# Eight transposes into a PSUM buffer of two banks, emptied by one copy of 1,024 columns, in a linear-attention and mixture-of-experts kernel

## The chip, the cores and the metric

The kernel runs on one core of one Trainium2 chip. The metric is the time of one execution on the device, in microseconds, as the median of several runs. Engine names in this text are those of the profile: PE is TensorE's matmul, PEld its weight load, DVE is VectorE, ACT is ScalarE, POOL is GpSimd, SP is SyncE, whose queue issues most DMAs.

## What is computed

Inputs: q, k, v, a_re, a_im of shape 4 (batch) x 8 (heads) x 768 (time) x 48; gate weights 384 x 8, noise, and eight experts' weights w1 (384 x 1024) and w2 (1024 x 384).

```python
scale = min(|a|, 0.999) / (|a| + 1e-6);  ar, ai = a_re*scale, a_im*scale
for t in range(768):                       # a complex state S of 48 x 48 for each batch and head
    S = (ar + i*ai)[:, None] * S + outer(k[t], v[t])
    y[t] = q[t] @ real(S)
x = y as 3072 rows of 384
logits = x @ w_gate + log1p(exp(x @ w_noise)) * noise
top 2 of 8 experts per row, softmax weights g
out[row] = sum over its 2 experts of g * (relu(x @ w1[e]) @ w2[e])
```

## The kernel before

The attention part takes the recurrence in chunks of 128 time steps: 6 chunks x 4 batches make 24 tiles (`NT`), and a group `g` is the 4 tiles of one chunk. A tile holds all 8 heads. Running products of a come from cumulative sums: PE multiplies logarithm and angle by triangular matrices (`p2t`, L250, and `p3`, L270, into the tile `cum`), and ACT takes exponentials and sines (`phase`, L199, with a load of another table, L198, at each switch between the two kinds). `p3q` (DVE, L282) makes from them q' and k' of a tile: 128 time steps by 8 heads by 112 numbers (`qh`, `kh`).

Then, for tile `n`:

- `tr_unit` (L286 to L294) transposes q' and k', so that the 112 numbers lie on partitions. Each call does 4 heads (a half): four PE transposes into one PSUM tile `ptr` of 4 x 128 columns, which is one bank, and one ACT copy of 512 columns into half of the SBUF tile `qT` or `kT`. There are four such calls for a tile: two halves of q', two halves of k'. The tile `ptr` has two buffers, as the pool `psA` has `bufs=2`.
- `sc_unit` (L302) multiplies k'T by q'T, 4 heads to a call, into `psc` (two buffers of one bank); DVE masks it into `am` (L303).
- `st_unit` (L312) makes the tile's addition to the state in `pG` (one bank), `y_unit` (L349, L351) the output in `pY` (one bank) from q'T and the state `z` and from `am` and v; ACT copies it to `xT` (L352).
- `x_unit`, `gate_logits` and `gate_dispatch` transpose the output back, find the two experts of each row and scatter the rows to the expert's places in DRAM by indirect DMAs (POOL, L413).

`cum` has two banks, `ptr` two, `psc` two, `pG` and `pY` one each: together the eight banks of PSUM.

The expert part then does, for each of 8 experts, transposes of the gathered rows (`x_T`, into `px`, L504; ACT casts, L506, and DVE takes the rest, L507), the first product (`mm1`, L519, into `ph`), and the second (`mm2`, L543). Its first pieces, expert 0 with 512 rows, run before the attention's PSUM pools close: `ps_tile` then gives `px` the buffers of `ptr` and `ph` those of `psc`.

The order of all this is not written out loop by loop. Every unit is put at a step by `at(step, function, ...)`, with offsets from the table `P`, and the units are traced in the order of these steps; a scheduler then places each engine's instructions by that priority and by when their operands and buffers are free. Each engine runs its own queue in the order that came out. The offsets of `tr_unit` are:

```python
at(n - P["tr"] + P["tk"] * i + P["th"] * half, tr_unit, n, i, half)   # tr=1.4, tk=0.2, th=0.05
at(n + P["sc"] + P["sh"] * half, sc_unit, n, half)                    # sc=-0.2, sh=0.05
at(n + P["st"], st_unit, n); at(n + P["y"], y_unit, n)                # st=0.05, y=0.2
```

Of the kernel before, what the change touches and what calls it, by code (L numbers as in the profile page):

```python
# [9 lines left out]
F32 = mybir.dt.float32  # L10
# [4 lines left out]
AF = mybir.ActivationFunctionType  # L15
# [62 lines left out]
def kernel(  # L78
# [8 lines left out]
    nc = tc.nc  # L87
# [28 lines left out]
    ident = cp.tile([128, 128], F32, name="ident")  # L116
# [47 lines left out]
    pa = ap.enter_context(tc.tile_pool(name="pa", bufs=1, side="right"))  # L164
# [5 lines left out]
    psA = ap.enter_context(tc.tile_pool(name="psA", bufs=2, space=PSUM))  # L170
# [112 lines left out]
                             QK[n][:, i, :].rearrange("p (h d) -> p h d", h=H)[:, None].to_broadcast([128, 2, H, D]),  # L283
                             tr)

    def tr_unit(n, i, half):  # L286
        x = (qh, kh)[i][n % NQ]
        store = (QT, KT)[i]
        if half == 0:
            store[n] = pa.tile([112, H, 128], F32, name=("qT", "kT")[i], bufs=2)  # L290
        p = psA.tile([128, 4, 128], F32, name="ptr")[0:112]
        for j in range(4):
            nc.tensor.transpose(p[:, j, :], x[:, 4 * half + j, :, :].rearrange("p r x -> p (r x)")[:, 0:112], ident)
        nc.scalar.activation(store[n][:, 4 * half:4 * half + 4, :], p, AF.Copy)  # L294

    def sc_unit(n, half):
        if half == 0:
# [128 lines left out]
    def at(step, f, *a):  # L426
        fill.setdefault(step, []).append((f, a))
# [37 lines left out]
    def ps_tile(name, bufs=2):  # L465
        if psB:
            return psB[0].tile([128, 512], F32, name=name, bufs=bufs)
        return psA.tile([128, 4, 128], F32, name={"px": "ptr", "ph": "psc"}[name]).rearrange("p a b -> p (a b)")


    def split(raw_t, hi, lo):
# [18 lines left out]
    def x_T(e, w):  # L490
        n = WIN[w][1]
        src_t = xga if w == 0 else xgb
        js = ((0, 1, 2, 3), (4, 5, 6))[w]
        if w == 0:
            GW[e] = mt([128, 7], F32, name="gw", bufs=2)
            OX[e] = mt([128, 7], U32, name="ox", bufs=2)
        nc.vector.tensor_copy(GW[e][:, js[0]:js[-1] + 1], src_t[:, :, DM + e])
        nc.vector.tensor_copy(OX[e][:, js[0]:js[-1] + 1], src_t[:, :, RNO])
        for kk in range(KD):
            x = XW[w, kk] = mt([128, 2, n], F32R, name=f"x{w}{kk}")  # L500
            p = ps_tile("px")
            for j in js:
                o = 128 * (j - js[0])
                nc.tensor.transpose(p[:, o:o + TW[j]], src_t[0:TW[j], j - js[0], kk * 128:(kk + 1) * 128],  # L504
                                    ident[0:TW[j], 0:TW[j]])
            nc.scalar.copy(x[:, 0, :], p[:, :n])  # L506
            nc.vector.tensor_tensor(x[:, 1, :], p[:, :n], x[:, 0, :].bitcast(F32), op=OP.subtract)  # L507

    def mm1(e, w, fs=range(KF)):
        n = WIN[w][1]  # L510
        for f in fs:

            h = mt([128, 2 * n], F32R, name=f"h{w}{f}")
            t = n % 128
            HT[w, f] = h[:, 0:n + t], h[:, n + t:]
            p = ps_tile("ph", 4)
            ms = [(i, j, kk) for kk in range(KD) for i, j in ((0, 0), (0, 1), (1, 0))]
            for m, (i, j, kk) in enumerate(ms):
                nc.tensor.matmul(p[:, :n], W1[kk][i][:, f * 128:(f + 1) * 128], XW[w, kk][:, j, :],  # L519
                                 start=(m == 0), stop=(m == len(ms) - 1))  # L520
            nc.scalar.activation(h[:, 0:n], p[:, :n], AF.Relu)  # L521
            for dst, a, b in ((n + t, 0, n - t), (n, n - t, n)):
                if a < b:
                    nc.vector.scalar_tensor_tensor(h[:, dst:dst + b - a], p[:, a:b], 0.0, h[:, a:b].bitcast(F32),  # L524
                                                   op0=OP.max, op1=OP.subtract)
# [9 lines left out]
    def mm2(e, w):  # L535
        for j in ((0, 1, 2, 3), (4, 5, 6) if e + 1 < E else (6, 4, 5))[w]:
# [8 lines left out]
            else:  # L545
# [15 lines left out]

    P = dict(la=10, p1=7, d1=1, p2=6, dt=0, ds=0, lqk=6, p3=4, d3=0, q=2, lv=5, xu=0.5, ss=3, gl=0, gd=0.25,
             tr=1.4, sc=-0.2, st=0.05, y=0.2, up=0.4, w1=18, w2=21, xt=23, m1=23.3, dm=0.2, co=6, hg=50,
             hx=50, hl=200, s0=(7, 5.5, 4.5), s1=(7.5, 6, 5), qd=0.05, tk=0.2, th=0.05, sh=0.05)
    pri = {gdis: P["hg"], x_unit: P["hx"], glog: P["hl"]}
    for g in range(NG):
        f = B * g + .5
# [8 lines left out]
        for j in range(B):  # L576
            n = B * g + j
# [5 lines left out]
    for n in range(NT):  # L583
        at(n + .5 - P["lv"], load_v, n)
        for i in range(2):
            for half in range(2):
                at(n - P["tr"] + P["tk"] * i + P["th"] * half, tr_unit, n, i, half)
        for half in range(2):
            at(n + P["sc"] + P["sh"] * half, sc_unit, n, half)
        at(n + P["st"], st_unit, n)  # L590
        at(n + P["y"], y_unit, n)
        at(n + P["up"], st_upd, n)
        at(n + .5 + P["xu"], x_unit, n)
        at(n + .5 + P["ss"], st_scale, n)
# [88 lines left out]
    nc.vector.tensor_add(flg[:, 1:2], flg[:, 1:2], flg[:, 0:1])  # L683
    nc.vector.tensor_add(flg[:, 1:2], flg[:, 1:2], ncnt)
    pfl = ps_tile("px")
    nc.tensor.matmul(pfl[0:1, 0:2], ones_f, flg, start=True, stop=True)
    flag = cp.tile([1, 2], I32, name="flag")
# [187 lines left out]
```

## Time and profile before

| | |
|---|---|
| median of 3 runs | 739.68 us (739.3 to 739.75) |
| the profiled execution | 739.76 us, of which the span from its first to its last instruction is 738.0 |
| attention tiles | about 32 to 257 us of the span |
| experts | from 257 us to the end |

The views that are used: busy time of each engine by stretches of the span; the view of one tile, which lists the instructions that touch it, what they waited for and who waited for them; the list of waits; groups of instructions by line and shape with their mean duration; and the timeline, in which each row is a run of equal instructions of one engine with its start, its length, its count and, in brackets, the idle time ahead of it and what ended that. An instruction that the program issues once for f32 operands stands as two passes in the trace where it is a product (L302, L312, L349, L351, L250, L270), and as one where it is a transpose (L293, L359, L504).

### The profile page before, as it was taken

What the parts mean: (1) busy time and instruction counts of PE and PEld (TensorE: products, weight loads), DVE (VectorE), ACT (ScalarE), POOL (GpSimd) and SP (SyncE); (2) the same over time, 40 slices, a digit from 0 to 9 for tenths busy, and PEclk for the clock granted to TensorE, in tenths of its full rate; (3) what the DMA queues carried; (4) which work ended last, traced back from release to release, by engine and by line L of the source; (5) the groups of instructions that cost most, each with busy time, mean ns of one, the idle gap of its engine ahead of it and who ended that gap; (6) DMA issues with size and microseconds to landing.
All of it is one profiled execution on the core that took longest, in us unless ns stands there. A gap on an engine that the chain in (4) does not pass through costs nothing. (4 is left out here: it accounts for less than half of the span.)

```text
span 738.0 us, 13470 instructions
## 1 busy us (share of the span) xinstructions
PE 699.7 (95%) x5184; PEld 622.5 (84%) x5184; DVE 411.3 (56%) x929; ACT 342.5 (46%) x609; POOL 166.1 (23%) x187
## 2 busy tenths in 40 slices
PE   0798989999999999999999999999999999999996
PEld 0377878878888879979988998998997998998995
DVE  5598888989899472553353344435525525435311
ACT  6899989798966430443133233223304403413300
POOL 2000005050506341032213123124024024122212
PEclk9899999999999999999999999999999999999999
DMA  7467876462457541271253244226226135031101
GB/s 284 118 222 189 263 218 239 132 219 46 155 143 238 201 165 74 81 239 51 97 172 106 87 139 147 75 98 202 75 88 208 43 115 191 28 108 54 51 33 34
DMA packets 64090, 100.18 MB, mean 136 GB/s; under 512 B 26490, under 2 KB 46129, under 8 KB 64016
## 3 DMA queue, kind: packets, MB, share of 16 engines
q1 hardware_dynamic: 54464, 71.68, 31.2%
q0 software_dynamic: 9552, 27.54, 10.7%
q8 instruction: 43, 0.70, 0.4%
q14 instruction: 31, 0.25, 0.1%
HBM read 68.55 MB, written 32.08 MB: 136 GB/s over the span
## 5 line engine op out<-in xcount | busy, mean ns | idle before, releaser
L543 PE MATMUL po<-w2h,h 128*128 128x384 f32 x768 | 201.8, 339 | 0.0
L519 PE MATMUL ph<-x,w1h 128*128 128x320 f32 (+1 forms) x720 | 192.4, 351 | 0.3 <-ACT x L506 0.3
L543 PEld LDWEIGHTS po<-w2h,h 128*128 128x128 f32 x768 | 139.9, 188 | 0.1
L519 PEld LDWEIGHTS ph<-x,w1h 128*128 128x128 f32 x720 | 126.7, 188 | 15.6 <-ACT x L506 0.5
L543 PE MATMUL po<-w2l,h 128*128 128x384 f32 x384 | 129.7, 338 | 0.0
L524 DVE SCALAR_TENSOR_TENSOR h<-ph,h 128x256 fp32r<-128x256 f32 (+2 forms) x184 | 74.2, 433 | 99.4 <-ACT h L521 99.4
L557 POOL DMA_INDIRECT out_dram<-ao,ox x56 | 55.7, 994 | 319.8 <-DVE ao L556 276.3
L519 PE MATMUL ph<-x,w1l 128*128 128x320 f32 (+1 forms) x360 | 125.5, 349 | 0.0
L521 ACT ACTIVATE h<-ph 128x320 fp32r<-128x320 f32 (+1 forms) x120 | 61.5, 512 | 119.0 <-PE ph L519 113.6
L556 DVE SCALAR_TENSOR_TENSOR ao<-po,gw,ao 128x384 f32<-128x384 f32 (+1 forms) x56 | 34.5, 616 | 134.0 <-PE po L543 133.0
L413 POOL DMA_INDIRECT xs<-xr,sl x48 | 53.7, 1118 | 200.6 <-DMA xd<-xr 108.6
L506 ACT CAST x<-px 128x320 fp32r<-128x320 f32 (+1 forms) x45 | 21.8, 502 | 126.8 <-PE px L504 125.9
L519 PEld LDWEIGHTS ph<-x,w1l 128*128 128x128 f32 x360 | 67.6, 188 | 7.3
L543 PEld LDWEIGHTS po<-w2l,h 128*128 128x128 f32 x384 | 72.1, 188 | 0.0
L530 POOL DMA_INDIRECT ao<-out_dram,ox x49 | 49.0, 1000 | 36.8 <-DMA out_dram<-ao,ox 24.0
L302 PE MATMUL psc<-qT,kT 112*128 112x128 f32 x384 | 53.3, 277 | 0.0
L472 ACT CAST w2h<-raw 128x768 fp32r<-128x768 f32 x32 | 25.3, 833 | 52.9 <-PE po L548 49.3
L302 PEld LDWEIGHTS psc<-qT,kT 112*128 112x128 f32 x384 | 47.7, 191 | 2.5 <-issue 1.3
L351 PE MATMUL pY<-am,v 128*48 128x128 f32 x384 | 42.6, 275 | 4.1 <-DVE am L303 4.1
L303 DVE TENSOR_TENSOR am<-psc,mask 128x512 f32<-128x512 f32 x48 | 32.6, 687 | 16.2 <-PE psc L302 16.1
L349 PE MATMUL pY<-qT,z 112*48 112x128 f32 x320 | 37.4, 276 | 0.0
L250 PE MATMUL cum<-t,tri_t 128*128 128x384 f32 x48 | 20.0, 545 | 17.6 <-ACT t L199 17.1
(206 smaller groups left out, 1019.6 us busy)
## 6 DMA issues: line engine op xcount, KB each, us to landing
raw<-in_moe_w_dram SPq DMA_DIRECT2D x24, 512.0 KB
raw<-in_moe_w_dram SPq DMA_DIRECT2D x32, 384.0 KB
qk<-in_qk_dram SPq DMA_DIRECT2D x24, 384.0 KB
xga<-xs SPq DMA_DIRECT2D x8, 800.0 KB
re<-in_a_dram SPq DMA_DIRECT2D x12, 384.0 KB
im<-in_a_dram SPq DMA_DIRECT2D x12, 384.0 KB
v<-in_v_dram SPq DMA_DIRECT2D x24, 192.0 KB
out_dram<-zero SPq DMA_DIRECT2D x12, 384.0 KB
```

Source lines behind the costliest of these rows:

```text
L302: nc.tensor.matmul(p[:, j, :], KT[n][:, h, :], QT[n][:, h, :], start=True, stop=True)
L303: nc.vector.tensor_mul(AM[n][:, 4 * half:4 * half + 4, :], p, mask[:, None, :].to_broadcast([128, 4, 128]))
L349: nc.tensor.matmul(o, Z[b][:, h, :], QT[n][:, h, :], start=True, stop=False, skip_group_check=True)
L351: nc.tensor.matmul(o, V[n][:, h, :], AM[n][:, h, :], start=not g, stop=True, skip_group_check=True)
L413: d = nc.gpsimd.indirect_dma_start(out=xs, out_offset=bass.IndirectOffsetOnAxis(ap=sl[:, kk, b:b + 1], axis=0), in_=XR[g][:, lo + b, :], i ...
L519: nc.tensor.matmul(p[:, :n], W1[kk][i][:, f * 128:(f + 1) * 128], XW[w, kk][:, j, :], start=(m == 0), stop=(m == len(ms) - 1))
L521: nc.scalar.activation(h[:, 0:n], p[:, :n], AF.Relu)
L524: nc.vector.scalar_tensor_tensor(h[:, dst:dst + b - a], p[:, a:b], 0.0, h[:, a:b].bitcast(F32), op0=OP.max, op1=OP.subtract)
L530: nc.gpsimd.indirect_dma_start(out=ao[j][0:w, :], out_offset=None, in_=out, in_offset=bass.IndirectOffsetOnAxis(ap=OX[e][0:w, j:j + 1], ax ...
L543: nc.tensor.matmul(p[:, :DM], HT[w, f][i][:, o:o + 128], W2[f // 2][k2][:, f % 2, :], start=(m == 0), stop=(m == len(ms) - 1))
L556: nc.vector.scalar_tensor_tensor(a, p[0:n, :DM], g, a, op0=OP.mult, op1=OP.add)
L557: nc.gpsimd.indirect_dma_start(out=out, out_offset=bass.IndirectOffsetOnAxis(ap=OX[e][0:n, j:j + 1], axis=0), in_=a, in_offset=None, bound ...
```

## The change

`tr_unit` loses its argument `half`: one call transposes all 8 heads of q' or k' into a `ptr` tile of 8 x 128 columns, which is two banks, and one ACT copy of 1,024 columns moves it to `qT` or `kT`. `ptr` now has one buffer, so that it takes the same two banks. `px` of the early `x_T` takes the first half of that one buffer. In the table `th` goes and `tk` is 0.4.

```diff
-    def tr_unit(n, i, half):
+    def tr_unit(n, i):
         x = (qh, kh)[i][n % NQ]
         store = (QT, KT)[i]
-        if half == 0:
-            store[n] = pa.tile([112, H, 128], F32, name=("qT", "kT")[i], bufs=2)
-        p = psA.tile([128, 4, 128], F32, name="ptr")[0:112]
-        for j in range(4):
-            nc.tensor.transpose(p[:, j, :], x[:, 4 * half + j, :, :].rearrange("p r x -> p (r x)")[:, 0:112], ident)
-        nc.scalar.activation(store[n][:, 4 * half:4 * half + 4, :], p, AF.Copy)
+        store[n] = pa.tile([112, H, 128], F32, name=("qT", "kT")[i], bufs=2)
+        p = psA.tile([128, H, 128], F32, name="ptr", bufs=1)[0:112]
+        for h in range(H):
+            nc.tensor.transpose(p[:, h, :], x[:, h, :, :].rearrange("p r x -> p (r x)")[:, 0:112], ident)
+        nc.scalar.activation(store[n], p, AF.Copy)
...
-        return psA.tile([128, 4, 128], F32, name={"px": "ptr", "ph": "psc"}[name]).rearrange("p a b -> p (a b)")
+        if name == "px":
+            return psA.tile([128, H, 128], F32, name="ptr", bufs=1).rearrange("p a b -> p (a b)")[:, 0:512]
+        return psA.tile([128, 4, 128], F32, name="psc").rearrange("p a b -> p (a b)")
...
-             hx=50, hl=200, s0=(7, 5.5, 4.5), s1=(7.5, 6, 5), qd=0.05, tk=0.2, th=0.05, sh=0.05)
+             hx=50, hl=200, s0=(7, 5.5, 4.5), s1=(7.5, 6, 5), qd=0.05, tk=0.4, sh=0.05)
...
-            for half in range(2):
-                at(n - P["tr"] + P["tk"] * i + P["th"] * half, tr_unit, n, i, half)
+            at(n - P["tr"] + P["tk"] * i, tr_unit, n, i)
```

The scheduler's order moves with it. Three places on PE, in which `x8` is the number of equal instructions in a row and the number behind `qh` or `kh` tells the two buffers of q' and k' apart.

The first tiles, on PE. Before:

```order
L293 MATMUL ptr<-ident,qh_123 112x128 x8
L312 MATMUL pG<-v,kh_125 48x48 x16
L293 MATMUL ptr<-ident,kh_125 112x128 x8
L293 MATMUL ptr<-ident,qh_124 112x128 x4
L302 MATMUL psc<-qT,kT 128x128
L293 MATMUL ptr<-ident,qh_124 112x128 x4
L302 MATMUL psc<-qT,kT 128x128 x3
L293 MATMUL ptr<-ident,kh_126 112x128 x4
```

and in the changed program:

```order
L292 MATMUL ptr<-ident,qh_123 112x128 x8
L311 MATMUL pG<-v,kh_125 48x48 x16
L292 MATMUL ptr<-ident,kh_125 112x128 x8
L292 MATMUL ptr<-ident,qh_124 112x128 x8
L301 MATMUL psc<-qT,kT 128x128 x8
L292 MATMUL ptr<-ident,kh_126 112x128 x8
```

Tile 1's transposes of q' now stand in one run right behind tile 0's of k', with nothing between them.

A late tile on PE, the last but two. Before, halves of k' and of the scores alternate:

```order
L293 MATMUL ptr<-ident,qh_123 112x128 x8
L302 MATMUL psc<-qT,kT 128x128 x4
L293 MATMUL ptr<-ident,kh_125 112x128 x4
L302 MATMUL psc<-qT,kT 128x128 x4
L293 MATMUL ptr<-ident,kh_125 112x128 x4
L349 MATMUL pY<-qT,z_566 48x128 x2
L351 MATMUL pY<-am,v 48x128 x2
```

In the changed program the next tile's place reads:

```order
L301 MATMUL psc<-qT,kT 128x128 x7
L292 MATMUL ptr<-ident,kh_126 112x128 x8
L348 MATMUL pY<-qT,z_638 48x128 x2
L350 MATMUL pY<-am,v 48x128 x2
L348 MATMUL pY<-qT,z_638 48x128 x2
L350 MATMUL pY<-am,v 48x128 x2
```

All eight scores of a tile now stand between the next tile's transposes of q' and of k', and the transposes of k' stand in one run ahead of the tile's output.

The start of the experts on PE. Before, seven of the first eight transposes of the gathered rows are one run, over both buffers:

```order
L504 MATMUL ptr<-ident,xga 128x128 x7
L399 LDWEIGHTS tri_b
L399 MATMUL cum<-ohs_3486,tri_b 128x8
L359 MATMUL cum<-ident,xT 128x128 x4
```

Now four, for the one buffer:

```order
L505 MATMUL ptr<-ident,xga 128x128 x4
L398 LDWEIGHTS tri_b
L398 MATMUL cum<-ohs_3390,tri_b 128x8
L358 MATMUL cum<-ident,xT 128x128 x4
```

The second group of transposes comes behind the first two products of `mm1`, which read the first group's result.

## Rows read from the trace of the kernel before

**Rows 1.** The page's first part: the span, and busy time, share and instructions of each engine.

```profile
span 738.0 us, 13470 instructions
PE 699.7 (95%) x5184; PEld 622.5 (84%) x5184; DVE 411.3 (56%) x929; ACT 342.5 (46%) x609; POOL 166.1 (23%) x187
```

**Rows 2.** Busy time of each engine by stretches (us from the span's start, then for each engine busy us and instructions, then the granted TensorE clock as a share, the DMA engines' busy share and GB/s).

```profile
50.00:100.00 50.00, 48.05 (x525) 38.82 (x525) 41.61 (x64) 46.26 (x82) 0.00 (x0) 1.00 0.68 203
100.00:150.00 50.00, 48.05 (x581) 40.65 (x577) 45.37 (x124) 42.12 (x80) 12.12 (x11) 1.00 0.65 204
150.00:200.00 50.00, 49.31 (x603) 42.60 (x603) 44.46 (x96) 45.87 (x82) 17.78 (x20) 1.00 0.44 137
200.00:250.00 50.00, 49.38 (x602) 43.15 (x600) 40.84 (x137) 32.81 (x67) 18.29 (x19) 1.00 0.64 202
...
262.00:738.00 476.00, 468.30 (x2590) 431.25 (x2590) 201.27 (x420) 132.65 (x234) 112.64 (x114) 1.00 0.33 106
```

**Rows 3.** The view of the tile `ptr`: its copies (count, then duration in ns least/median/most), what the engines that touch it waited for, and who waited for it.

```profile
L294 ACT ACTIVATE qT<-ptr x48: 586/597/661, 34.0 to 246.1; 112x512 f32<-112x512 f32 x48
L294 ACT ACTIVATE kT<-ptr x48: 577/597/670, 36.8 to 248.7; 112x512 f32<-112x512 f32 x48
...
  ACT kT L294: 1.7, 5
...
  ACT kT L294: 9.2, 17
  ACT qT L294: 1.9, 4
```

**Rows 4.** The waits of PE and of its weight loads from 30 to 262 us (in total, times, longest).

```profile
PE pY L351 <- DVE am L303: 4.1, 5, 1.3
PE cum L270 <- ACT ee L199: 3.8, 1, 3.8
PE cum L399 <- DVE ohs L392: 1.9, 3, 1.3
PE ptr L293 <- ACT kT L294: 0.5, 2, 0.3
...
PEld ptr L293 <- issue: 6.3, 29, 1.0
PEld ptr L293 <- ACT kT L294: 1.2, 3, 0.5
```

**Rows 5.** Groups by line and shape up to 340 us: copies on ACT of other widths (count, busy us, mean ns of one, idle before).

```profile
L360 ACT COPY xr<-cum 128x384 f32<-128x384 f32 x24 | 11.6, 484 | 5.2 <-PE cum L359 4.2 <-DMA raw<-in_moe_w_dram 0.9
L352 ACT ACTIVATE xT<-pY 128x512 f32<-128x512 f32 x24 | 14.3, 598 | 6.5 <-PE pY L351 6.5
L199 ACT ACTIVATE t<-t 128x768 f32<-128x768 f32 x36 | 29.7, 849 | 0.3
L472 ACT CAST w1h<-raw 128x1024 fp32r<-128x1024 f32 x6 | 6.2, 1045 | 0.0
```

**Rows 6.** The timeline of a late tile, 237 to 242.5 us, PE and ACT.

```profile
237.66 1.09 PE L293 MATMUL ptr<-ident,qh 128*112 128x128 f32 x8
238.34 1.08 ACT L294 ACTIVATE qT<-ptr 112x512 f32<-112x512 f32 x2
238.58 1.06 PE L302 MATMUL psc<-qT,kT 112*128 112x128 f32 x8
239.47 0.60 PE L293 MATMUL ptr<-ident,kh 128*112 128x128 f32 x4
...
240.81 0.60 PE L293 MATMUL ptr<-ident,kh 128*112 128x128 f32 x4
241.34 0.43 PE L349 MATMUL pY<-qT,z 112*48 112x128 f32 x4
241.45 0.60 ACT L294 ACTIVATE kT<-ptr 112x512 f32<-112x512 f32 x1 [0.58 <-PE ptr L293]
```

**Rows 7.** The timeline of a tile in the middle, 149 to 156 us, in which ACT is behind.

```profile
148.81 1.08 PE L293 MATMUL ptr<-ident,kh 128*112 128x128 f32 x8
149.50 0.60 ACT L294 ACTIVATE kT<-ptr 112x512 f32<-112x512 f32 x1 [1.30 <-PE ptr L293]
149.99 0.93 ACT L199 ACTIVATE t<-t,b_eps 128x768 f32<-128x768 f32 x1
150.15 0.65 PE L293 MATMUL ptr<-ident,qh 128*112 128x128 f32 x4 [0.25 <-ACT kT L294]
150.94 1.28 ACT L198 ACT_TABLE_LOAD   x1
152.23 1.58 ACT L199 ACTIVATE t<-t 128x768 f32<-128x768 f32 x2
153.72 0.58 ACT L294 ACTIVATE kT<-ptr 112x512 f32<-112x512 f32 x1
```

**Rows 8.** The timeline of two more pairs of copies, 96 to 116 us, ACT.

```profile
101.44 1.11 ACT L294 ACTIVATE kT<-ptr 112x512 f32<-112x512 f32 x2
104.55 1.14 ACT L294 ACTIVATE qT<-ptr 112x512 f32<-112x512 f32 x2
```

**Rows 9.** The timeline of PE in the first tiles, 40 to 62 us.

```profile
43.74 0.64 PE L351 MATMUL pY<-am,v 128*48 128x128 f32 x8 [0.89 <-DVE am L303]
45.94 1.41 PE L312 MATMUL pG<-v,kh 128*48 128x48 f32 x30 [0.47 <-DVE z L324]
58.10 1.50 PE L312 MATMUL pG<-v,kh 128*48 128x48 f32 x32 [0.65 <-DVE z L324]
```

**Rows 10.** The start of the experts, 256.5 to 262.5 us.

```profile
257.19 0.98 PE L504 MATMUL ptr<-ident,xga 128*128 128x128 f32 x7
258.36 0.57 ACT L506 CAST x<-ptr 128x512 fp32r<-128x512 f32 x1
259.01 0.69 DVE L507 TENSOR_TENSOR x<-ptr,x 128x512 fp32r<-128x512 f32 x1
261.07 0.66 PE L504 MATMUL ptr<-ident,xga 128*128 128x128 f32 x4
```

**Rows 11.** Short stretches of the start, columns as in the second group.

```profile
30.00:35.00 5.00, 5.00 (x23) 3.06 (x22) 5.00 (x7) 4.97 (x11) 0.00 (x0) 0.50 0.56 106
35.00:40.00 5.00, 4.75 (x56) 4.45 (x55) 5.00 (x9) 3.31 (x8) 0.00 (x0) 0.96 0.70 139
60.00:65.00 5.00, 3.89 (x32) 3.01 (x30) 5.00 (x7) 4.56 (x12) 0.00 (x0) 1.00 0.52 91
```

## The prediction

> **What bounds the kernel now.** Start from the page's first part [rows 1]: PE is busy for 95% of the span, ACT for 46%. Then the stretches [rows 2]. From 262 us on PE is busy for 468.3 of 476 us and ACT for 132.7, so the experts are PE's alone, and the change touches nothing there but their first transposes. Whatever it does is done before, in the 24 attention tiles, and moves the end of the program by as much. In that part PE's busy share is 96 to 99%, but ACT stands at 46.3 of 50 us in one stretch and 45.9 in another, DVE at 41 to 45. So three engines are close to full, and the question is which of them is waited for last. The waits answer it [rows 4]: between 30 and 262 us PE's matmuls stood still for named reasons for about a dozen us in all, mostly for the masked scores (4.1 us) and one exponential (3.8 us). For the copies that the change merges, PE stood still twice, 0.5 us, and its weight loads three times, 1.2 us. The other way round the copies waited for the transposes 21 times, 9.2 and 1.9 us [rows 3]. PE is the engine to watch, then, and today the copies hardly delay it: ACT's relief by itself has little to give, and a new wait of PE would be paid nearly in full.
>
> **Term 1, the copies.** 96 copies of 512 columns become 48 of 1,024. One of 512 takes 597 ns [rows 3]; 384, 512, 768 and 1,024 columns in other copies and functions take 484, 598, 849 and 1045 ns [rows 5]. From 512 on, 512 more columns at 0.77 ns each (768 to 1,024) give 0.99 us, at 0.89 ns (384 to 512) 1.05; I take 1.03. Two copies that follow each other take 1.08, 1.11 and 1.14 us from the first's start to the second's end [rows 6, 8], so a merged pair saves 0.05 to 0.11 us; at 0.08 the 48 pairs save 3.8 us of ACT. Where a copy stands alone, 0.597 x 2 - 1.03 = 0.16 us goes, at most 7.9 us for all. What reaches the end is that part in which PE waits for ACT in its turn. ACT is above 90% busy in two of the four attention stretches [rows 2], so I count half: -1.9 us, with 0 (all of it hidden under PE) and -3.8 as bounds.
>
> [...]
>
> **Term 2, TensorE's turns.** Changing from another kind of work to a run of transposes costs PE a little: weight loads of `ptr` began late 29 times with nothing that released them, 6.3 us, 0.22 us each [rows 4]. The order before enters a run of `ptr` transposes 81 times from other work, the changed one 70 times, since halves no longer alternate with scores. 6.3 / 81 x 11 = -0.9 us; bounds 0 and 11 x 0.22 = -2.4.
>
> **Term 3, one buffer.** This is what the change adds. Before, the third half could be transposed while the first was copied. Now the transposes of k' wait until the whole of q' is copied, and those of the next q' until k' is. In a quiet tile [rows 6] the last of four transposes starts 0.33 us behind the first (240.81), and the copy starts 0.64 behind the first, so 0.2 us after PE is free for other work; the copy is 1.03; and PE begins 0.05 us behind a copy's end (150.10 to 150.15 [rows 7]). So PE needs 1.28 us of other work between two runs of transposes, if ACT is free. Such work can be counted from the changed order: a transpose is 0.11 us, eight passes of scores 0.89 (238.58 to 239.47 [rows 6]), so all eight heads, 16 passes, 1.79, and 32 passes of `pG` 1.5 [rows 9].
>
> There are 47 hand-overs between the 48 runs. Thirty-one have 2.2 us or more of other work between them, up to 7, and hide the copy with room to spare. Thirteen have 1.29 to 1.85 us, typically the scores of one tile between the next tile's q' and k'. Three have less than the need: 0.00, 0.44 and 0.99 us. The three cost 1.28 + 0.84 + 0.29 = 2.4 us; the first falls into the filling of the pipeline, where PE stands still anyway for the masked scores and the state (0.89 and 0.47 us [rows 9]), so I count 1.1. Of the thirteen, four are in the last tiles, where copies start at once; they cost nothing. The other nine have some 0.5 us of room, and lose where ACT has an operation of 0.9 us or more ahead of the copy. In 75 of 96 copies ACT did not wait for PE [rows 3], and where it is behind it can be far behind: the second half of k' is transposed by 149.9 us and copied at 153.72, behind an activation, a table load and two more activations [rows 7]. But such long stretches meet the wide gaps of the changed order more than the thin ones. I take 0.2 us each, 1.8 us. Together +2.7; bounds 0 (ACT always free, fill hidden) and 2.4 + 9 x 0.5 = +6.9.
>
> Queued behind a waiting transpose is all of PE's work, as its queue runs in order; next in line are the scores, then DVE's mask, then the output.
>
> **Term 4, the experts' start.** Three groups of four transposes now share one buffer that is free only when ACT's cast and DVE's subtraction are through: 0.57 and 0.69 us [rows 10]. The order puts two products and other work between them, some 1.35 to 1.45 us, against a need near 1.5. I take +0.3, bounds 0 and +0.8. Before, the third group already had to wait until 261.07 [rows 10].
>
> The edits to `tk` and `th` have no cost of their own: they make the order that the terms count. DMA issues on SP and POOL are the same in number, and follow DVE and the tiles.
>
> **Sum.** -1.9 - 0.9 + 2.7 + 0.3 = +0.2 us on the profiled execution's 739.76, so 740.0; that execution stands 0.08 us above the median of the runs shown, which is no difference. About 0.2%, 1.5 us, is what a measurement of this kernel can tell from no change. So the forecast is no measurable change, 738.2 to 741.2, with a chance of 0.35.
>
> **Rivals.** *The relief arrives whole.* If ACT is what the attention tiles wait for in truth, through chains that the waits name otherwise (scores masked late because k' was copied late), then all of term 1 counts, term 2 at its estimate, and hand-overs hide under the scores as in the last tiles: -3.8 - 0.9 + 0.6 = 735.7 us. For it: ACT's 46 of 50 us, and copies up to 4 us behind [rows 2, 7]. Against it: 1.7 us of PE waits on copies. Chance 0.33.
>
> *The single buffer becomes the new wait.* It costs from the point at which ACT starts a copy more than about 0.5 us late at the thirteen thin hand-overs. Term 3 and 4 at their bounds, with relief and turns worth 2 us, give 739.8 + 6.9 + 0.8 - 2 = 745.5; half-way, 743. For it: PE waits for nothing else so directly. Against it: today many reuses of a buffer have as little room, and PE lost only 1.7 us by them [rows 4]. Chance 0.28. [...]
>
> *The merged copy is no cheaper.* If reading across two banks costs as much as two copies, 1.19 us, ACT gains nothing, and each copy is 0.11 us longer than an adjacent pair: half of 48 x 0.11 = +2.6 in place of -1.9, and thirteen hand-overs longer by 0.16: 740.0 + 4.5 + 2.1 = 746.6. No row shows a copy over two banks. Chance 0.03.
>
> *TensorE's clock falls.* [...] Chance 0.01. [...]
>
> **Numbers.** Faster by more than 0.2%: 0.33. Within: 0.35. Slower: 0.28 + 0.03 + 0.01 = 0.32. The range takes in the first rival's price with the forecast's lower bounds, and the second's up to its full price: 734.5 to 745.5. The forecast case's own range is 738.2 to 741.2.
>
> **What would show it.** Right: 48 copies of 0.99 to 1.05 us; ACT's busy time down by 3 to 8 us; PE's waits on `qT` and `kT` copies up from 1.7 to some 3 to 5 us; experts from about the same moment, 257 us. Wrong on term 3: those waits above 7 us, at the hand-overs with scores alone between. Wrong on term 1: waits of PE on masked scores and exponentials fall by several us, and the experts start before 254 us.

## The result

The changed kernel takes 746.03 us (median of 4 runs, 744.36 to 746.38), the kernel before 739.49 us (738.53 to 739.75) beside it: ratio 1.0087, 95% interval 1.007 to 1.0103. It is 6.5 us slower, above the range's upper end of 745.5. The profiled execution took 746.38 us with a span of 744.6.

**The profile after.** The page's first part, against [rows 1]:

```profile
span 744.6 us, 13412 instructions
PE 700.2 (94%) x5184; PEld 621.9 (84%) x5184; DVE 411.6 (55%) x929; ACT 338.5 (45%) x561; POOL 174.9 (23%) x187
```

ACT has 48 instructions and 4.0 us less, PE's work is the same. The view of the tile `ptr`, against [rows 3]:

```profile
L293 ACT ACTIVATE qT<-ptr x24: 1012/1024/1047, 33.5 to 243.6; 112x1024 f32<-112x1024 f32 x24
L293 ACT ACTIVATE kT<-ptr x24: 1002/1023/1056, 35.7 to 246.8; 112x1024 f32<-112x1024 f32 x24
...
  ACT kT L293: 4.0, 5
  ACT qT L293: 3.9, 3
```

The merged copy takes 1.02 us, and PE and its weight loads sat idle for such copies 7.9 us (4.0 and 3.9), before 1.7 for k' [rows 3] and 0.2 for q'. Still the attention is no longer. From the last copy of k' of the second tile to that of the last tile (41.85 to 248.65 us before, 40.61 to 246.84 after, the lines below) it is 206.80 us before and 206.23 after. What else differs up to here is the start of the execution, and that is not the change's: in the other runs, of both kinds of kernel, the second tile's copy stands anywhere from 40.3 to 42.0 us. Before:

```profile
41.85 0.59 ACT L294 ACTIVATE kT<-ptr 112x512 f32<-112x512 f32 x1
248.65 0.60 ACT L294 ACTIVATE kT<-ptr 112x512 f32<-112x512 f32 x1 [0.74 <-PE ptr L293]
```

and after:

```profile
40.61 1.02 ACT L293 ACTIVATE kT<-ptr 112x1024 f32<-112x1024 f32 x1 [0.17 <-PE ptr L292]
246.84 1.02 ACT L293 ACTIVATE kT<-ptr 112x1024 f32<-112x1024 f32 x1 [1.83 <-PE ptr L292]
```

The time goes at the seam, where the attention ends and the experts begin. The waits from 30 to 262 us, against [rows 4]:

```profile
POOL xr L339 <- DMA xs<-xr,sl: 13.3, 4, 5.8
DVE gw L498 <- DMA xga<-xs: 8.6, 1, 8.6
PE pY L350 <- DVE am L302: 8.0, 2, 7.2
PEld ptr L292 <- issue: 5.8, 25, 1.3
PE ptr L292 <- ACT kT L293: 1.7, 2, 1.1
PE ptr L292 <- ACT qT L293: 1.5, 1, 1.5
```

PE's one wait of 7.2 us is for the last tile's masked scores. The timeline of the seam (PE, PEld and DVE, with the issue of one load from SP's queue, SPq) shows who stands ahead of them. It stands against [rows 10], where the experts' first transposes began at 257.19 and their third group at 261.07:

```profile
251.52 0.86 PE L301 MATMUL psc<-qT,kT 112*128 112x128 f32 x6
...
253.23 0.39 PE L348 MATMUL pY<-qT,z 112*48 112x128 f32 x4
254.76 0.33 SPq L442 DMA_DIRECT2D xga<-xs  x1
259.08 0.17 DVE L498 COPY gw<-xga 128x4 f32<-128x4 f32 x1 [8.57 <-DMA xga<-xs]
260.03 0.68 DVE L302 TENSOR_TENSOR am<-psc,mask 128x512 f32<-128x512 f32 x1
260.77 0.67 PE L350 MATMUL pY<-am,v 128*48 128x128 f32 x4 [7.15 <-DVE am L302]
262.22 1.12 PE L505 MATMUL ptr<-ident,xga 128*128 128x128 f32 x4
266.18 0.66 PE L505 MATMUL ptr<-ident,xga 128*128 128x128 f32 x4
268.44 0.60 PE L505 MATMUL ptr<-ident,xga 128*128 128x128 f32 x4
```

Read it from DVE: `gw`, a copy of 0.17 us out of the rows gathered for expert 0 (`x_T`, L498), stands in DVE's queue ahead of the mask, and waits 8.57 us for the gather. Before it waited too, 2.38 us:

```profile
250.45 0.33 SPq L443 DMA_DIRECT2D xga<-xs  x1
254.71 0.17 DVE L497 COPY gw<-xga 128x4 f32<-128x4 f32 x1 [2.38 <-DMA xga<-xs]
255.66 0.68 DVE L303 TENSOR_TENSOR am<-psc,mask 128x512 f32<-128x512 f32 x1
```

The last scores were done at 252.38 (251.52 + 0.86), and their mask began only at 260.03, 7.65 us later, behind `gw`. The load itself did not get slower: from its issue to the start of `gw` it is 4.26 us before and 4.32 after. It was issued 4.3 us later.

Then the clock. Stretches of after, columns as in [rows 2]:

```profile
250.00:255.00 5.00, 3.62 (x56) 3.04 (x50) 0.51 (x1) 0.74 (x2) 1.94 (x2) 1.00 0.35 126
255.00:260.00 5.00, 0.00 (x0) 0.00 (x0) 0.59 (x5) 0.22 (x1) 0.00 (x0) 0.80 0.48 164
260.00:265.00 5.00, 4.23 (x31) 3.52 (x31) 4.09 (x25) 1.98 (x5) 0.00 (x0) 0.52 0.01 2
```

Behind a stop of 7 us PE works at a mean granted clock of 0.52 in these 5 us, and four transposes of the rows take 1.12 us instead of 0.66. In stretches of 1 us each from 245 to 295 us, PE's idle time is 8.15 us in all and the busy time lost to the lower clock (busy share times one less the clock, added up) 2.0 us; before the two were 1.45 and 0. That is +8.7 us (8.15 - 1.45 + 2.0); less 1.2 for the earlier start and 0.6 for the attention it is 6.9, against the 6.6 by which the spans differ.

### The profile page after: what moved, and what is told of

It reads as the page before. It is cut to its first block, busy times and chain, and to the rows that moved or that the text cites. A ratio compares the mean times of both kernels' runs of the same rounds, so it can differ in the third digit from the quotient of the medians.

```text
span 744.6 us, 13412 instructions
## 1 busy us (share of the span) xinstructions
PE 700.2 (94%) x5184; PEld 621.9 (84%) x5184; DVE 411.6 (55%) x929; ACT 338.5 (45%) x561; POOL 174.9 (23%) x187
## 5 line engine op out<-in xcount | busy, mean ns | idle before, releaser
L412 POOL DMA_INDIRECT xs<-xr,sl x48 | 63.0, 1312 | 193.4 <-DVE am L302 123.8
L301 PE MATMUL psc<-qT,kT 112*128 112x128 f32 x384 | 50.9, 277 | 0.5 <-ACT kT L293 0.5
L350 PEld LDWEIGHTS pY<-am,v 128*48 128x48 f32 x384 | 29.3, 124 | 12.7 <-DVE am L302 8.9
```

Of the source, the lines that this page charges most:

```text
L301: nc.tensor.matmul(p[:, j, :], KT[n][:, h, :], QT[n][:, h, :], start=True, stop=True)
L350: nc.tensor.matmul(o, V[n][:, h, :], AM[n][:, h, :], start=not g, stop=True, skip_group_check=True)
L412: d = nc.gpsimd.indirect_dma_start(out=xs, out_offset=bass.IndirectOffsetOnAxis(ap=sl[:, kk, b:b + 1], axis=0), in_=XR[g][:, lo + b, :], i ...
```

## Experiments

Two theories stood at first: **A**, the loss is a late gather and DVE's queue behind it; **B**, it is the hand-overs of the single buffer. The gather's chain is: gate of group 4 on DVE (slots `sl`, L408), eight scatters on POOL (L412), the load of `xga` on SP, `gw`. The slots are the places in DRAM to which the rows of the group go; a scatter needs them. Counted from the second tile's last copy of k', the slots stand 1.9 us later than before in the changed kernel's profile, but the first scatter of group 4 stands 5.7 us later (201.75 against 196.04). The other 3.8 are POOL's: that scatter stood behind a memset of POOL (L339) that waited for group 3's scatters, 5.77 us, until 241.52. In a_gw and a_free, whose programs are the same at this place, the memset ended near 239.3 and the first scatter began 1.5 to 1.8 us behind the slots, so this share differs from run to run.

**a_gw.** `gw` and `ox` behind the last mask in DVE's queue:

```diff
-        nc.vector.tensor_copy(GW[e][:, js[0]:js[-1] + 1], src_t[:, :, DM + e])
-        nc.vector.tensor_copy(OX[e][:, js[0]:js[-1] + 1], src_t[:, :, RNO])
+        c = nc.vector.tensor_copy(GW[e][:, js[0]:js[-1] + 1], src_t[:, :, DM + e])
+        d = nc.vector.tensor_copy(OX[e][:, js[0]:js[-1] + 1], src_t[:, :, RNO])
+        if (e, w) == (0, 0):
+            for i in (c, d):
+                tc.add_manual_dep(i.ins, LAST_AM[0].ins.name, mybir.DependencyInfo(
+                    mybir.DependencyClass.NoSync, mybir.DependencyReason.DATA), reason="behind the last mask")
```

> The changed kernel with one thing moved on DVE: the two small copies of expert 0's gathered rows (gw, ox out of xga) stand behind the last tile's mask instead of ahead of it. Theory A (the 6.5 us come from DVE's queue standing behind a late gather, not from the buffer): PE's wait of 7.2 us on the last am goes, the last tile's output is made at about 254 us; the gather itself still lands at about 259, so the experts start near 260 instead of 262.2 and the clock falls less: 741 to 744 us in place of 746.0. Theory B (hand-overs of the single buffer): 745.5 to 746.5, since nothing on the copies is touched.

Measured: 746.21 us, ratio 1.0106 (1.0092 to 1.0121). No gain, and outside A's 741 to 744; B's 746.5 is nearer. In its profile PE then waited for the gather itself, 0.76 us, and 1.6 us for `ohs` (the rows' choices of experts as ones and zeros, which PE sums to places), which DVE made behind `gw`.

**a_pad.** The memset and copy for group 5's `xr` behind group 4's scatters on POOL:

```diff
-            nc.gpsimd.memset(XR[g][:, :, RNO + 1:ROW], 0.0)
-            nc.gpsimd.tensor_copy(XR[g][:, :, RNO], tokid[:, g])
+            if g + 1 < NG:
+                pad_xr(g)
...
             at(B * g + hi + .5 + P["gd"], load_x, 0, 0, xga)
+            at(B * g + hi + .5 + P["gd"] + .05, pad_xr, NG - 1)
```

`pad_xr` holds the two lines, and for group 5 orders them behind the last scatter.

> The changed kernel with one thing moved on POOL: the memset and the copy that prepare the row buffer xr of group 5 (the last) stand behind group 4's scatters instead of ahead of them, so that these scatters don't wait for group 3's scatters to land. Theory A: group 4's first scatter at about 238 us instead of 242.4, the gather lands by 256, no wait over 3 us of PE on am, experts from about 256 to 257.5: 737.5 to 740.5 us. Theory B: 744.5 to 746.5, as the copies are as they were.

Measured: 744.73 us, 1.0087 (1.0072 to 1.0103). The scatters start at 240.0 instead of 242.4 us, and not at 238; the time is outside A's 737.5 to 740.5 and within B's range. The ratio is as without the move; its interval leaves room for about 1 us either way.

**a_both** and the control **b_both**: both moves, in the changed kernel and in the one before.

> The changed kernel with both moves, on DVE and on POOL. Theory A: the attention's own gain of about 1.8 us (the last copy of k' at 246.8 us against 248.6) comes through to the end: 736.5 to 739 us. Theory B: 744 to 746.5.

> The kernel before (halves, two buffers) with both moves, the control. Its gather was waited for by 2.4 us on DVE, and PE by about 1 us. Theory A: 0 to 1.5 us faster than before, 738 to 739.5, and the changed kernel with both moves is 0.5 to 2.5 us faster than this one. Theory B: this one is 5 to 7 us faster than the changed kernel with both moves.

Measured: 743.94 us, 1.0062 (1.0047 to 1.0076), and 737.05 us, 0.9977 (0.9965 to 0.9988). The control is 1.4 us faster than the kernel before, as theory A said. The changed kernel is far outside A's 736.5 to 739: 6.9 us are still between the two, within the 5 to 7 that theory B had asked for. So the memset and the place of `gw` are not the cause, only carriers, and B was not yet out. The gather still lands late (`gw` waits 3.1 us), and the first to the ninth transpose of the rows takes 9.7 us (3.9 before).

**a_free and b_free** take the gather out of the question, and leave out the right rows for expert 0's start. From here A is called theory **S** (all of the loss is the late gather at the seam), and a third theory stands beside it, **C** (the single buffer at the experts' start). Expert 0's first rows come from `v`:

```diff
-            at(B * g + hi + .5 + P["gd"], load_x, 0, 0, xga)
+            at(B * g + hi + .5 + P["gd"], load_free)
+    def load_free():
+        nc.sync.dma_start(xga[:, :, 0:DM], v[0:4].rearrange("j p r -> p j r"))
+        nc.sync.dma_start(rw, x3[0, 0:512, DM:RNO + 1].rearrange("(p j) r -> p j r", j=4))
...
+    at(P["m1"] + .5 + P["dm"] * 4 + .01, weights_free)
```

`weights_free` makes `gw` and `ox` from `rw`.

> The changed kernel, but the 512 rows that expert 0 begins with come from the input v instead of from the scattered rows, so that their load waits for no scatter; only the nine columns with gate weight and row number still come from there, into a small tile of their own, and are copied behind the fifth group of first products. Left out: expert 0's first 512 rows are not the right ones. PE's order is that of the changed kernel, word for word. Theory S (seam: all of the loss comes from the gather landing late against the end of the attention, and from what PE's stop there entails): no stop on PE over 1 us between 245 and 262 us, granted clock 1.00 throughout, 737.0 to 739.5 us, within 1.2 us of the same edit made to the kernel before. Theory B (hand-overs of the single buffer in the attention): 5 to 6 us above that one, 742 to 744. Theory C (the single buffer at the experts' start, term 4): 2 to 5 us above it, seen as 6 us or more from the first to the ninth transpose of the rows, against 3.9 before.

> The kernel before with the same edit: expert 0's first 512 rows from the input v. Left out: those rows are not the right ones. All theories: it loses its own waits of 2.4 us on DVE and 1 us on PE, so 736 to 738.3 us.

Measured: 739.49 us, 1.0017 (1.0007 to 1.0026), and 737.24 us, 0.9983 (0.9971 to 0.9994). Theory B falls, with its 742 to 744: the same 48 hand-overs, in the same order on PE, and the one bank at the experts' start together cost 2.25 us (about 1.4 to 3.6 by the two intervals). Theory S's range of 737 to 739.5 is just met, but not its 1.2 us over b_free; theory C's 2 to 5 us are, though the first to the ninth transpose take 5.93 us, just under its 6. So a part of the loss is not the gather's. PE's waits from 245 to 270 us in a_free say which:

```profile
PE psc L533 <- DVE h L538: 0.9, 1, 0.9
...
PE cum L398 <- DVE ohs L391: 0.7, 1, 0.7
```

The first does not occur in b_free, and the second is 0.3 there. Both belong to the seam and the experts' start.

**b_px** is term 4 alone, the three groups of transposes in one bank:

```diff
+        one = ps_tile("px") if (e, w) == (0, 0) else None
...
-            p = ps_tile("px")
+            p = ps_tile("px") if one is None else one
```

> The kernel before, but the three groups of transposes of expert 0's first rows share one PSUM tile of one bank, as in the changed kernel; the attention keeps its two buffers. Theory S: 0 to 0.8 us over before (the bounds of term 4), 738.5 to 739.5. Theory C: 2 to 5 us over before, 740.5 to 743.5.

Measured: 740.12 us, 1.0028 (1.0016 to 1.004), so +1.9 us (1.2 to 3.0). Theory S's bound of 0.8 is wrong, theory C's sign is right, at the lower end. PE in b_px:

```profile
256.32 0.66 PE L505 MATMUL ptr<-ident,xga 128*128 128x128 f32 x4
257.79 0.18 PE L399 MATMUL cum<-ohs,tri_b 128*128 128x8 bf16 x1 [0.81 <-DVE ohs L392]
...
260.14 0.66 PE L505 MATMUL ptr<-ident,xga 128*128 128x128 f32 x4
...
262.40 0.60 PE L505 MATMUL ptr<-ident,xga 128*128 128x128 f32 x4
...
266.67 0.74 PE L520 MATMUL psc<-x,w1h 128*128 128x512 f32 x2 [0.92 <-DVE h L525]
```

No wait for the buffer itself stands there: the order had put products between. But with the third group at 262.40 two sums of `mm1` are left open over both `psc` buffers, they are finished one behind the other, and the third has to wait for ACT and DVE to empty the first, 0.92 us. Before, PE waited 0.49 us for `ohs` at this place and not at all for that `h`. The two make 1.2 of the 1.9 us; for the rest no wait was found. That reading is from the rows; it was not tried by itself.

**a_g2**: a_both, with `gw` and `ox` (in `weights_of`) behind the last subtraction `s` of `x_T`:

```diff
+        if (e, w) == (0, 0):
+            for i in weights_of(e, js, src_t):
+                tc.add_manual_dep(i.ins, s.ins.name, mybir.DependencyInfo(
+                    mybir.DependencyClass.NoSync, mybir.DependencyReason.DATA), reason="behind the transposes")
```

> The changed kernel with both moves of the earlier runs, but the two small copies out of the gathered rows stand on DVE behind the last subtraction of the rows' transposes, so that nothing of the gate's chain for tiles 20 to 22 queues behind the gather. Theory S: PE's wait of 1.6 us for ohs goes, the stop is the 2 us for the gather alone, the clock falls later or not at all: 739.5 to 742 us in place of 743.9. Theory B: 743.5 to 744.5.

Measured: 740.94 us, 1.0037 (1.0024 to 1.0051); as theory S said. The wait for `ohs` is gone, the clock stays at 1.00, and PE's wait for the gather is left:

```profile
257.10 0.66 PE L517 MATMUL ptr<-ident,xga 128*128 128x128 f32 x4 [1.71 <-DMA xga<-xs]
```

Its control **b_g2** (the same two moves before the change) has none. Its forecast names two more theories on why the gather is late: **O**, the order of DVE's queue; **M**, the merged buffer and copy themselves.

> The kernel before with the two moves (memset behind group 4's scatters, the two small copies behind the rows' transposes): the control for the run beside it, and the version that would beat both kernels. Both theories: 736 to 737.5 us. Theory O: the changed kernel with the moves and the priority is 1.5 to 2.5 us above it, the price of the single buffer at the experts' start. Theory M: 3.5 to 4.5 us above.

Measured: 737.14 us, 0.9987 (0.9977 to 0.9996). The single bank (1.9 us, b_px) and PE's wait above (1.7) add up to 3.6 of the 3.8 us between the two. That is an addition across kernels and chips, and was not tried.

**Why the gather is late: b_tk4 and b_hg20.** The order of DVE's queue at the slots of tiles 16 to 18, before:

```
L401 TENSOR_TENSOR pos<-cum,base_run 128x24
L72 TENSOR_TENSOR ga3t<-ga3oh,ga3w 128x48
...
L473 TENSOR_TENSOR w2l<-raw,w2h 128x768
L409 TENSOR_REDUCE sl<-ga3oh 128x6
L473 TENSOR_TENSOR w2l<-raw,w2h 128x768
L375 COPY lz<-cum 128x16
L282 TENSOR_TENSOR kh_126<-qk,tr 128x2x8x48
```

and in the changed kernel:

```
L474 TENSOR_TENSOR w2l<-raw,w2h 128x768
L69 RECIPROCAL ga3w<-ga3e 128x3
L400 TENSOR_TENSOR pos<-cum,base_run 128x24
L70 TENSOR_TENSOR ga3w<-ga3w 128x3
L282 TENSOR_TENSOR kh_126<-qk,tr 128x2x8x48
L72 TENSOR_TENSOR ga3t<-ga3oh,ga3w 128x48
...
L474 TENSOR_TENSOR w2l<-raw,w2h 128x768
L374 COPY lz<-cum 128x16
L408 TENSOR_REDUCE sl<-ga3oh 128x6
```

One more subtraction of the weights (`w2l`) and tile 22's k' (`kh`), 0.95 us each in the trace, now stand ahead of the slots. **b_tk4** has the kernel before with the change's steps alone:

```diff
-             hx=50, hl=200, s0=(7, 5.5, 4.5), s1=(7.5, 6, 5), qd=0.05, tk=0.2, th=0.05, sh=0.05)
+             hx=50, hl=200, s0=(7, 5.5, 4.5), s1=(7.5, 6, 5), qd=0.05, tk=0.4, th=0.0, sh=0.05)
```

**b_hg20** has the kernel before with another priority of the gate's chain, 20 in place of the table's `hg=50`:

```diff
-    pri = {gdis: P["hg"], x_unit: P["hx"], glog: P["hl"]}
+    pri = {gdis: 20, x_unit: P["hx"], glog: P["hl"]}
```

Both were first run on one of two chips on which every kernel took some 33 us more, the kernel before too (771.64 and 771.2 us), all of it by the end of the attention. PE had no wait for the first gather there, and `gw` at most 0.4 us, so that they tell nothing on this question (1.0011, 0.9991 to 1.0031, and 1.0014, 0.9999 to 1.0029). On another chip:

> The kernel before with the steps of the change alone (tk 0.4, th 0), once more, since on the chip of the run before every kernel stood still for some 33 us. Slots of tiles 16 to 18 stand 6.9 us of DVE work ahead of the last mask (9.4 before, 7.4 in the changed kernel; estimates from the order). Theory O (the place of group 4's gate chain in DVE's queue sets when the gather lands): 740.5 to 745 us. Theory M (the merged buffer and copy make the gather late): 737 to 739.5, as before.

> The kernel before with the priority of the gate's chain at 20, once more. Slots 7.2 us of DVE work ahead of the last mask. Theory O: 740.5 to 745 us. Theory M: 737 to 739.5.

Measured: 742.06 us, 1.0054 (1.0039 to 1.0069), and 741.96 us, 1.0049 (1.0029 to 1.0068). Theory O, twice: with halves, two buffers and the old copies, a moved order of DVE's queue with later slots costs 3.9 and 3.8 us. Neither order is the changed kernel's: b_tk4's slots stand later than its own. So the steps alone are enough to make the gather late; whether merged units at the old steps would do it too was not tried. The waits from 245 to 270 us of b_tk4_2 show the same two waits, shorter:

```profile
DVE gw L497 <- DMA xga<-xs: 4.0, 1, 4.0
...
PE pY L351 <- DVE am L303: 2.6, 1, 2.6
```

**a_g2hg**: a_g2 with `hg=75` (`pri = {gdis: 75, ...}`), by which the slots stand 9.3 us of DVE work ahead of the last mask again. On a slower chip it gave 1.0012 (0.9988 to 1.0036); on the other:

> The changed kernel with both moves and the priority of 75, once more. Slots 9.3 us of DVE work ahead of the last mask. Theory O: the gather no longer ends last, and only the single buffer at the experts' start is left: 738 to 740 us. Theory M: 740.5 to 741.5.

Measured: 743.96 us, 1.0074 (1.0058 to 1.009), slower than a_g2 by 3 and outside both theories' ranges. The part on the gather came true: the first transposes of the rows start at 256.39 behind the last output, with no wait. But some 20 us later the same thing happens with the rows of the next window, whose `gw` stands ahead of a subtraction of `mm1`, and the clock falls again, to 0.50 from 281 to 284 us. Waits from 250 to 296 us:

```profile
DVE gw L500 <- DMA xgb<-xs: 3.4, 1, 3.4
PE psc L536 <- DVE h L541: 3.4, 2, 2.6
```

**a_hg75** (the changed kernel with `hg=75` alone), **a_g3** (a_g2hg with all such copies behind the transposes) and its control **b_g3** (the same in the kernel before, with `hg=50`) were only run on the slower chips.

> The changed kernel with the same number at 75: the slots stand 9.5 us of DVE work ahead of the last mask, as in the kernel before (7.4 in the changed one), and the rows' copy to DRAM goes ahead of two weight loads on SP. Theory O: the gather lands earlier, 740 to 743 us; what is left over before is the single buffer at the experts' start, about 2 us, and the wait of the memset for group 3's scatters where it still ends last. Theory M: 745 to 746.5.

> The changed kernel with the memset behind group 4's scatters, the priority of 75, and for every expert the two small copies out of the gathered rows behind those rows' transposes, so that nothing on DVE stands behind a gather that it doesn't need. In the run before without the last, the first gather was no longer waited for, but the copy for the next window held DVE 3.4 us, PE stood still for 2.6 and the clock fell. Theory O: no stop of PE over 1.5 us from 245 to 295 us, clock 1.00 there, 738 to 740 us. Theory M: 740.5 or more.

> The kernel before with the memset behind group 4's scatters and all the small copies behind the transposes. Both theories: 736 to 737.5 us, which would beat both kernels. Theory O: the changed kernel with the same and the priority is 1.5 to 2.5 us above it, the single buffer at the experts' start. Theory M: 3.5 us or more above.

Measured, against 771.64 and 771.2 us of the kernel before: 1.0053 (1.0034 to 1.0073), 1.0011 (0.9984 to 1.0037) and 1.0003 (0.9977 to 1.0029). They don't tell the theories apart, since PE did not wait there for the first gather, in the kernel before either. The 0.5% of a_hg75 is clear of noise, and its cause is open. That the priority helps the changed kernel is therefore shown for the first gather's wait alone, in the one profile of a_g2hg_2, and not for the time.

The profiles on the faster chips in one table. The slots are the start of `sl` of tiles 16 to 18, counted from the second tile's last copy of k'; the wait is that of `gw` or of PE for the load of `xga`; the last column adds up PE's idle time and time lost to the clock from 245 to 295 us, as above. Each is one execution, and need not be the median one (a_gw's was the fastest of six).

| kernel | ratio | slots, us | wait for the gather, us | PE idle + clock, us |
|---|---|---|---|---|
| before | 1 | 195.1 | 2.4 | 1.5 + 0 |
| b_g2 | 0.9987 | 194.4 | 0 | 0.4 + 0 |
| b_both | 0.9977 | 194.4 | 0 | 0.4 + 0 |
| b_px | 1.0028 | 195.2 | 2.6 | 3.0 + 0 |
| b_hg20_2 | 1.0049 | 196.7 | 4.3 | 3.3 + 0 |
| b_tk4_2 | 1.0054 | 198.1 | 4.0 | 2.8 + 1.6 |
| changed | 1.0087 | 197.0 | 8.6 | 8.2 + 2.0 |
| a_gw | 1.0106 | 197.3 | 1.7 | 3.3 + 1.7 |
| a_pad | 1.0087 | 197.5 | 4.5 | 4.0 + 1.7 |
| a_both | 1.0062 | 197.5 | 3.1 | 4.7 + 3.2 |
| a_g2 | 1.0037 | 197.5 | 1.7 | 2.6 + 0 |
| a_g2hg_2 | 1.0074 | 195.8 | 0 | 4.3 + 1.7 |
| a_free | 1.0017 | 197.4 | taken out | 1.7 + 0 |
| b_free | 0.9983 | 194.6 | taken out | 0.3 + 0 |

The fastest is b_both, 737.05 us, with b_g2 beside it within their intervals: nothing of the change, and the memset and `gw` out of the way.

## Why the prediction was wrong

- **Term 1, right.** 1.02 us for 1.03; ACT's busy time fell by 4.0 us for 3.8. How much of that reached the end, put at half, no run isolates.
- **Term 2, right in sign.** Late weight loads of `ptr`: 5.8 us in 25 for 6.3 in 29, so -0.5 for -0.9.
- **Term 3, near in its sum by luck, wrong in its places.** The 1.7 us before are PE's own stops and those of its weight loads; counted the same way the waits for k' and q' became 7.9 us, where 3 to 5 were forecast and more than 7 was to show the term wrong. Of that PE's matmuls stood still 3.2 us, in three stops. The first, 1.1 us at 36.8, is the hand-over with no work between. The second, 1.5 us at 65.8, stands behind a wide gap, one of those counted as hidden: q' was transposed by 54.9 us and copied only at 64.7, behind other work of ACT. The third, 0.5 us at 73.1, is a thin one. At the nine thin hand-overs priced at 0.2 us each PE did not stop for a copy, and nowhere after 102 us. Yet the waits did not lengthen the attention: up to the last tile PE's waits for masked scores fell from 3.1 to 0.9 us, and PE stood idle 5.3 us from 42 to 246 us, 6.6 before. The 3.8 us for the exponential [rows 4] are there in both kernels. Terms 1 to 3 together were put at -0.1 (term 3's own 1.1 and 1.8 make 2.9 and not 2.7, so rather +0.1, and 740.2 for the forecast); from the second to the last tile the attention measured -0.6, and +0.4 in a_free against b_free (206.69 and 206.33).
- **Term 4, too small.** +0.3 with bounds 0 and +0.8; b_px measures +1.9 (1.2 to 3.0). The step counted PE's wait for the buffer, found 1.35 to 1.45 us of cover for it, and was right on that. It did not follow the order on: by the rows of b_px, two sums are left open, PE waits 0.9 us for DVE's `h`, and 0.3 us more for `ohs`, as four transposes stand ahead of it where seven stood. The other 0.7 us of the 1.9 stay open.
- **The step that failed:** "The edits to `tk` and `th` have no cost of their own: they make the order that the terms count. DMA issues on SP and POOL are the same in number, and follow DVE and the tiles." They do follow DVE, and DVE's order had moved at the one place where a transfer is waited for. The terms counted the new order on PE alone. That such a move alone makes the gather late is shown by b_tk4_2 and b_hg20_2. For its price in the changed kernel there are two estimates, both twice that of term 4 or a little more: 4.0 us (2.9 to 5.1, from b_tk4_2's ratio, whose order is not the changed kernel's), and 6.5 less the 2.25 that is left without the gather, 4.3. With term 4's 1.9, 4.0 makes 5.9 of the 6.5; the intervals are some 1 us wide on either side. There was little room for it: before, DVE waited 2.4 us for the gather already.
- **Rivals.** The single buffer as the new wait (745.5) and the merged copy that is no cheaper (746.6) both come near in number, by mechanisms that the runs speak against: a_free keeps the buffer in the attention and at the experts' start, and is 2.25 us over b_free; and the copy takes 1.02 us, not 1.19. TensorE's clock did fall, to 0.50, but between the program's start and its end once, at the seam, and that took 2.0 us.

Open is why a_pad and a_gw gained nothing in the median although their profiles show shorter waits. The clock is a part of it: a_gw's profiled execution (742.32 us, the fastest) has a mean granted clock of 0.991 and its five others 0.988 to 0.990, and a_pad's slower ones 0.989 to 0.990 where its faster have 0.992 to 0.994. Open too is what the merged copy would give with steps that leave DVE's order alone; that was not tried.

## What to carry to other kernels

Where a change moves the steps of a scheduler, follow the new order on each queue to the next transfer that something waits for, not only on the engine that is full: here the slots stood behind two more pieces of 0.95 us on DVE, some 16 us ahead of PE's stop, and with the kernel before, moved orders of that kind cost 3.8 and 3.9 us. Look in the queues for short instructions that need late data, as `gw`: what stands behind them waits too, here the mask, which began 7.65 us after its scores were done. Moving one is no cure by itself: with the memset's move it gave 1.4 us in the kernel before, and alone nothing in the changed one, where PE then waited for the gather itself. And in giving up a second PSUM buffer, count on to what the later results hold open, not only the wait for the buffer: in b_px no wait for the buffer stands, but one of 0.92 us for DVE's `h`.

## What the runs showed of the hardware

- A copy out of two PSUM banks cost ACT nothing extra here: 1.02 us for 1,024 columns of 112 partitions, and 1.045 us for a cast of 1,024 columns on 128 partitions out of SBUF [rows 5].
- A stop of some 3 us did not always lower the clock here. In b_hg20_2 PE waited 2.9 us at the seam and the clock stayed at 1.00; in b_tk4_2 it waited 2.6 us, and a little later, when PE was busy again, the clock was 0.50. In a_gw it fell to 0.50 behind two stops of 0.76 and 1.64 us. Nor need it be the same in each execution: four others of b_hg20_2 are slower, with a mean clock of 0.988 to 0.990 against 0.992 in the profiled one, so that it may have fallen there. Stretches of b_tk4_2:

```profile
257.00:259.00 2.00, 0.73 (x12) 0.61 (x12) 1.51 (x7) 0.44 (x2) 0.00 (x0) 1.00 0.00 0
259.00:261.00 2.00, 1.84 (x14) 1.38 (x11) 1.83 (x18) 1.28 (x3) 0.00 (x0) 0.65 0.01 4
261.00:263.00 2.00, 2.00 (x16) 1.29 (x15) 1.40 (x7) 1.06 (x2) 0.00 (x0) 0.50 0.00 0
```

and of b_hg20_2:

```profile
255.00:257.00 2.00, 0.64 (x12) 0.61 (x12) 1.47 (x8) 0.45 (x2) 0.00 (x0) 1.00 0.00 0
257.00:259.00 2.00, 1.62 (x18) 1.23 (x13) 1.90 (x15) 1.72 (x4) 0.00 (x0) 1.00 0.02 4
259.00:261.00 2.00, 2.00 (x20) 1.44 (x18) 1.58 (x7) 0.51 (x2) 0.00 (x0) 1.00 0.00 0
```

- One and the same scatter on POOL took 1.67 or 4.35 us: group 3's first one took 1.67 in the kernel before and in b_both, which have the old copies, and 4.34 to 4.35 in the changed kernel, a_pad, a_both and a_g2hg_2, which have the merged one. In the kernel before, four loads of weights were issued from 0.9 us ahead of it on (220.07), in the changed one from 0.4 us behind its start (220.75); whether that is the cause was not tried. Timeline of POOL, before:

```profile
220.96 1.67 POOL L413 DMA_INDIRECT xs<-xr,sl  x1 [20.58 <-ACT xT L352]
235.12 0.12 POOL L340 MEMSET xr<- 128x28 f32 x1 [2.33 <-DMA xs<-xr,sl]
```

and after:

```profile
220.38 4.35 POOL L412 DMA_INDIRECT xs<-xr,sl  x1 [19.67 <-ACT w1h L473]
241.52 0.12 POOL L339 MEMSET xr<- 128x28 f32 x1 [5.77 <-DMA xs<-xr,sl]
```
